# Order of batch 1's theta stage, three more conversion buffers and separate last stores in a fused attention and mixing kernel

## The chip, the cores and the metric

The kernel runs on one core of one Trainium2 chip. The metric is the device time of one execution in microseconds (us), lower is better. The core's engines are TensorE (PE in the rows, with PEld for its weight loads), VectorE (DVE), ScalarE (ACT), GpSimd (POOL) and SyncE (SP), which here only issues DMA transfers. Each engine works through its own list of instructions in order; semaphores make one wait for another.

## What is computed

The reference has three parts, one behind the other, on two batches of 768 tokens with 512 channels (8 heads of 64). Its core:

```python
def _attn_ref(q, k, v, proj):          # q, k, v: [2, 8, 768, 64]
    q_bucket = bits of (q @ proj > 0); k_bucket = bits of (k @ proj > 0)
    scores = where(q_bucket == k_bucket, q @ k.T / sqrt(D), -1e9)
    return softmax(scores) @ v
def _moe_ref(x, w_ch1, w_ch2):
    u = x + real(fft(fft(x, axis=1), axis=2))
    un = (u - mean(u)) / sqrt(var(u) + 1e-06)
    return u + relu(un @ w_ch1) @ w_ch2
def _moe2_ref(x, w_theta, w_tok_r, w_tok_i, w_ch):
    theta = x @ w_theta
    zr, zi = x * cos(theta), x * sin(theta)
    y = w_tok_r @ zr + w_tok_i @ zi    # over the 768 tokens
    u = x + y
    return u + relu(u @ w_ch)
```

The weights of the last two parts are float64 in the inputs, the result is float32.

## The kernel before

**Staging.** Attention of batch 0, then attention of batch 1 beside the Fourier sums and the MLP of batch 0, then those of batch 1 beside the `theta` stage of batch 0, and at the end the late stages, which the change is about: the last MLP group `mlp2(1, 2)`, the `theta` stage of batch 1, and the token sums and channel products of both batches in halves of 384 output tokens. Matrix products are made from a high and a low half of each operand (`h` and `l` at the end of a name), three products for one.

**Order.** Nobody writes the engines' lists by hand. Each stage is a Python generator; `timed(gen, t0, dt)` (L910) runs it and gives each of its steps a priority, a due time of `t0` plus `dt` for each step, through `at(us)` (L131), and the tile scheduler of the language (L1167) merges all steps into one list for each engine, by its own simulation of time. `sooner(us)` makes some steps due earlier, here the update of `u` at the end of `mlp2`. `t0 = T["m1"] + 124` (L1041) is the due time at which the late stages start.

**theta (L814).** For each of 6 tiles t of 128 tokens PE transposes the tile of `u` into PSUM (`psf`); ACT copies it to `xs`, which SP stores to a DRAM buffer `xT` for later, and to the high half `xh`; DVE makes the low half `xl` by a subtraction. Twelve matmuls with `wthh` and `wthl` give theta in PSUM. Then come `nn` (ACT, POOL: the number of whole turns), `rr` (DVE, POOL: the rest), two sines on ACT, and the products zr and zi with their halves in the buffers named `x`, `u`, `za`, `zb`, `zc`. Tiles t = 2 and t = 5 of batch 1 need the update of `u` at the end of `mlp2(1, 2)`: `u<-psm,u` on DVE.

**Conversion of weights (from_f64 L169, conv32 L191, conv_tok L1016).** A chunk of a float64 weight is loaded by SP into a buffer `r64` (`r` in the rows) of a ring `cvs`; two ACT steps (`r<-r,chalf` and `r<-r`) and one DVE step make float32 of it; ACT copies the high half (`w1h`, `wtx` or `wchh`) and POOL subtracts for the low half (`w1l`). The ring has `NCV = 3` buffers, so the load of a chunk waits until the chunk three before it has been used by ACT and POOL. The token weights have 12 chunks of 384 columns for each half of the output tokens (`conv_tok(0)`, `conv_tok(1)`), `wch` has four of 512.

**tok_sum (L855) and tok_out (L889).** The first makes a half's token sums: 36 matmuls for each of four channel blocks, in `psm` or `psf`, added to `xt`, which is loaded back from `xT`. The second multiplies by `wch`, adds the relu (`xt<-psm,xt` on DVE) and stores two channel blocks of `xt` at a time.

**Late calls and their due times.** The last two chunks of half 0 at t0 − 14; `theta(1)` at t0; `tok_sum(0, 0)` at t0 + 20; `wch` at t0 + 22; `tok_sum(1, 0)` at t0 + 40 beside the chunks of half 1; `tok_out(0, 0)` at t0 + 56; the rest up to `tok_out(1, 1)` at t0 + 90 and `tok_out(0, 1)` at t0 + 100.

Of the kernel before, what the change touches and what calls it, by code (L numbers as in the profile page):

```python
# [9 lines left out]
F32 = mybir.dt.float32  # L10
# [5 lines left out]
AF = mybir.ActivationFunctionType  # L16
# [17 lines left out]
def f(t):  # L34
    return t.bitcast(F32)
# [35 lines left out]
def fused_kernel(ctx, tc, A, out):  # L71
# [3 lines left out]
    def pool(name, bufs=1, **kw):  # L75
        return tc.alloc_tile_pool(name=name, bufs=bufs, **kw)
# [10 lines left out]
    def stt(eng, out, in0, in1, op, scale=1.0):  # L87
# [5 lines left out]
    T = dict(  # L93
        pet='dpd', dup=1, c2=0, c0=46, cx=0, wm=6, gf=1, o2=0, xs=1, sb=2, al=[['p', 2], ['p2', 3], ['pt', 3]], cs='v', g0=1,
        lg=[[0, 2], [2, 4], [4, 6]], ub=2, pace0=1.6, lead=60, f0=50.0, w1=60.0, w1s=1.0, b1=115, pace1=2.6,
        w2=100.0, w2s=1.0, m0=170.0, f1=190.0, th=240.0, m1=290.0, z0=330.0, wt=300.0, n0=8, n1=16, k0=12, k1=16, c1=46, i0=40, i1=[20, 10],
        ne=42, es=150, ld='ss', lc='s', ps=[[0, 3], [0, 5], [1, 0], [1, 5]])
    P3 = ((0, 0), (0, 1), (1, 0))

# [714 lines left out]
    def theta(b, wth, zt):  # L814
        x2 = u_t[b]
        for t in range(NT):
            c = slice(128 * t, 128 * t + 128)
            pt = PS1()
            for kd in range(4):
                PE.transpose(pt[:, 128 * kd:128 * kd + 128], x2[:, t, 128 * kd:128 * kd + 128], ident)  # L820
            xs = zt([128, 4, 128], F32, "xs")
            AC.activation(out=xs, in_=pt.rearrange("p (k n) -> p k n", k=4), func=AF.Copy)
            SY.dma_start(out=xTd[b][:, :, c], in_=xs)
            xh = zt([128, 4, 128], F32R, "xh")
            xl = zt([128, 4, 128], F32R, "xl")
            pk = pt.rearrange("p (k n) -> p k n", k=4)
            AC.activation(out=xh, in_=pk, func=AF.Copy)
            V.tensor_tensor(out=xl, in0=pk, in1=f(xh), op=ALU.subtract)
            xx = (xh, xl)
            th = PS1()  # L830
            n = 0
            for kd in range(4):
                for a, k in P3:
                    mm(th, xx[a][:, kd], wth[k][:, kd], n == 0, n == 11)
                    n += 1
            nn = zt([128, DM], F32, "nn")
            AC.activation(out=nn, in_=th, func=AF.Identity, scale=1.0 / TWO_PI, bias=c_mag)
            PL.tensor_scalar(out=nn, in0=nn, scalar1=1.0, scalar2=-MAGIC, op0=ALU.mult, op1=ALU.add)
            rr = zt([128, DM], F32, "rr")
            V.scalar_tensor_tensor(out=rr, in0=nn, scalar=-PC1, in1=th, op0=ALU.mult, op1=ALU.add)  # L840
            V.scalar_tensor_tensor(out=rr, in0=nn, scalar=-PC2, in1=rr, op0=ALU.mult, op1=ALU.add)
            PL.tensor_scalar(out=rr, in0=rr, scalar1=3.1415925, scalar2=-3.1415925, op0=ALU.min, op1=ALU.max)
            V.tensor_scalar(out=nn.bitcast(U32), in0=rr.bitcast(U32), scalar1=0x7FFFFFFF, scalar2=None, op0=ALU.bitwise_and)
            AC.activation(out=rr, in_=rr, func=AF.Sin)
            AC.activation(out=nn, in_=nn, func=AF.Sin, scale=-1.0, bias=c_pi2)
            for r, trig in enumerate((nn, rr)):
                stt(V if r else PL, trig, trig, x2[:, t], ALU.mult)
                zh, zl = z_t[b][r]
                AC.activation(out=zh[:, t], in_=trig, func=AF.Copy)
                stt(PL if r else V, zl[:, t], trig, f(zh[:, t]), ALU.subtract)  # L850
            yield
# [34 lines left out]
            split(ps, kd)  # L886
            yield

    def tok_out(b, half, wch, kx):  # L889
        c = slice(TH * half, TH * half + TH)  # L890
        xt, uh, ul = kx
        uu = (uh, ul)
        for m in range(4):
            ps = PS1()
            n = 0
            for kd in range(4):
                for k, a in P3:
                    mm(ps[:, 0:TH], wch[k][:, kd, 128 * m:128 * m + 128], uu[a][:, kd], n == 0, n == 11)
                    n += 1
            V.scalar_tensor_tensor(out=xt[:, m], in0=ps[:, 0:TH], scalar=0.0, in1=xt[:, m], op0=ALU.max, op1=ALU.add)  # L900
            if m % 2:
                SY.dma_start(out=out[b, 128 * m - 128:128 * m + 128, c].rearrange("(k p) t -> p k t", p=128),
                             in_=xt[:, m - 1:m + 1])
            yield
# [90 lines left out]
    def zt(shape, dt, tag):  # L995
        n = turn.get(tag, 0)
        turn[tag] = n + 1
        return mk(zts[n % len(zts) if tag in ("nn", "rr") else 0], shape, dt, tag)
# [27 lines left out]
    ln_p.release()  # L1026
    m_p.release()
    w2_p.release()
    z1_p = pool("z1")
    z_t[1] = [[zz(u0_p, "u"), zz(z1_p, "za")], [zz(z1_p, "zb"), zz(z1_p, "zc")]]  # L1030
    wx_p = pool("wx")
# [9 lines left out]
    t0 = T["m1"] + 124  # L1041
    timed(conv_tok(0, 10), t0 - 14, 1)
    now[0] = "f"
    timed(theta(1, wth, zt), t0, 1)
    now[0] = "m"
    k0 = operands(xt_p, xt_p)
    timed(tok_sum(0, 0, wt, k0), t0 + 20, 2)
# [19 lines left out]
    timed(tok_sum(0, 1, wt, k1), t0 + 80, 2)  # L1067
    now[0] = "f"
    timed(tok_out(1, 1, wch, k0), t0 + 90, 1)
    timed(tok_out(0, 1, wch, k1), t0 + 100, 1)  # L1070
    for p in (xt1_p, wc_p, zb_p, u1_p, xt_p, wx_p, z1_p, dr_p, ring["f"][0][0], ring["m"][1][0], ring["m"][0][0], w1_p, x_p, u0_p, cv_p, const):
        p.release()


# [99 lines left out]
```

## Time and profile before

| | us |
|---|---|
| median of 3 runs | 740.17 (737.42 to 740.52) |
| the profiled execution | 742.22 |
| span in its profile | 740.5 |
| PE busy | 672.8 |
| PE weight loads busy (beside PE) | 515.0 |
| DVE busy | 401.4 |
| ACT busy | 376.4 |
| POOL busy | 371.2 |

The profile records one execution. Its own time is 742.22 us; the span from the first to the last recorded instruction is 740.5 us, with a mean granted clock of 0.965. A row of the timeline gives start, duration, engine, line, operation, written tile, read tiles and shape; in square brackets stands the idle time of the engine just before and what ended it. Nearly all instructions come from two helper lines, L62 and L64, so the tile names tell what an instruction is. Buffer numbers are left out in the rows (`r_6585` is `r`) but not in the order listings below. A "x2" behind a row means two like instructions in a row. The late stages are the last 190 us or so.

### The profile page before, as it was taken

How to read it: one execution, taken by the hardware profiler on the slowest of the kernel's cores; microseconds unless marked ns; L12 is line 12 of the kernel's file. 1: busy time of each engine (PE TensorE's matmuls, PEld its weight loads, DVE VectorE, ACT ScalarE, POOL GpSimd, SP SyncE). 2: the span in 40 equal slices, each digit the busy share in tenths (PEclk: the TensorE clock that was granted, in tenths of full speed). 3: DMA queues.
4: the chain of work that ended last, by engine and by line, in shares of the span. 5: the costliest groups of instructions: out<-in, count | busy, mean ns of one | idle time of the engine just before them, and what ended most of it. 6: DMA issues, size and time to landing. Idle time of an engine off the chain costs nothing.

```text
span 740.5 us, 13468 instructions
## 1 busy us (share of the span) xinstructions
PE 672.8 (91%) x5424; PEld 515.0 (70%) x5424; DVE 401.4 (54%) x649; ACT 376.4 (51%) x603; POOL 371.2 (50%) x312
## 2 busy tenths in 40 slices
PE   5798988778868897999999999999999799989997
PEld 2365566666747654786687675686584798989997
DVE  1466777778899556642394871254321366552222
ACT  2465554867898788764222260354325555562000
POOL 2777879589687888885450110134313155831000
PEclk9999999969789999999999999999999999999999
DMA  9886867469799999786550160010005511561202
GB/s 331 183 167 145 154 115 143 97 176 202 194 227 232 237 235 263 153 142 117 107 175 1 29 165 1 15 43 15 1 2 152 181 44 30 178 185 49 86 1 85
DMA packets 161438, 93.69 MB, mean 127 GB/s; under 512 B 137056, under 2 KB 147552, under 8 KB 161376
## 3 DMA queue, kind: packets, MB, share of 16 engines
q1 hardware_dynamic: 159440, 86.27, 49.9%
q0 software_dynamic: 1936, 6.57, 2.5%
q8 instruction: 42, 0.69, 0.4%
q14 instruction: 20, 0.16, 0.1%
HBM read 49.82 MB, written 6.29 MB: 76 GB/s over the span
## 4 chain that ended last, share of the span: by engine, by line
PE 42%; issue 10%; POOL 10%; DMA 9%; ACT 6%; DVE 4%; SPq 0%; POOLq 0%; ACTq 0%; DVEq 0%
PE psm L62 28%; PE psf L62 10%; DMA r<-in_wtok 4%; DMA r<-in_w 2%; POOL w1l L62 2%; ACT r L62 2%; POOL p L62 2%; PE pss L62 2%; POOL pt L62 2%; PE pso L62 2%; DMA r<-in_wch 1%; DMA x<-p 1%; ACT p L62 1%; ACT stk L62 1%; POOL w2l L62 1%
## 5 line engine op out<-in xcount | busy, mean ns | idle before, releaser
L62 PE MATMUL psm<-unT,w1h 128*128 128x256 f16 x768 | 130.1, 274 | 1.6 <-DVE u L62 1.4
L62 DVE SCALAR_TENSOR_TENSOR r<-r 128x512 uint32<-128x512 uint32 (+1 forms) x64 | 66.7, 1047 | 73.3 <-ACT r L62 61.4
L62 PE MATMUL psm<-unT,w1l 128*128 128x256 f16 x384 | 105.1, 274 | 0.0
L62 PEld LDWEIGHTS <-w1h 128*128 128x128 f16 (+1 forms) x774 | 75.2, 98 | 17.2 <-issue 6.3
L62 POOL TENSOR_TENSOR w1l<-r,w1h 128x384 fp32r<-128x384 f32 (+1 forms) x36 | 41.4, 1163 | 59.0 <-ACT w1h L62 58.9
L62 PEld LDWEIGHTS <-hh 128*128 128x128 f16 x384 | 36.9, 98 | 42.7 <-issue 1.1
L62 ACT ACTIVATE r<-r,chalf 128x512 uint32<-128x512 uint32 (+1 forms) x64 | 46.1, 721 | 38.3 <-DMA r<-in_wtok 20.5
L64 PE MATMUL pss<-stk 64*128 64x384 f32 (+1 forms) x288 | 58.4, 492 | 5.9 <-ACT p L64 3.0
L62 PE MATMUL pss<-stk 128*128 128x384 f32 x192 | 50.0, 388 | 11.9 <-ACT stk L62 6.6
L62 POOL TENSOR_TENSOR p<-p,p 128x768 f16<-128x768 f32 x32 | 53.4, 1672 | 12.9 <-ACT p L62 11.4
L62 PE MATMUL psm<-w2h,hl 128*128 128x512 f16 x192 | 59.7, 380 | 0.0
L62 PE MATMUL psm<-w2l,hh 128*128 128x512 f16 x192 | 59.4, 379 | 0.0
L62 PE MATMUL psm<-w2h,hh 128*128 128x512 f16 x192 | 59.3, 380 | 0.0
L62 DVE TENSOR_REDUCE nm<-pss 128x1 f32<-128x768 f32 x48 | 44.9, 946 | 20.5 <-PE pss L62 20.4
L64 DVE TENSOR_REDUCE nm<-pss 128x1 f32<-128x768 f32 x48 | 43.6, 950 | 22.5 <-PE pss L64 22.5
L62 ACT ACTIVATE p<-pss,nm 128x768 f32<-128x768 f32 x48 | 42.7, 895 | 21.7 <-DVE nm L62 20.2
L62 DVE SCALAR_TENSOR_TENSOR hl<-psm,hh 128x512 f16<-128x512 f32 x48 | 32.9, 685 | 37.8 <-ACT hh L62 37.7
L62 ACT ACTIVATE hh<-psm 128x512 f16<-128x512 f32 x48 | 28.3, 590 | 46.5 <-PE psm L62 46.4
L62 PEld LDWEIGHTS pss<-stk 128*128 128x128 f32 x192 | 35.3, 209 | 15.8 <-ACT stk L62 7.7
L62 PEld LDWEIGHTS <-w1l 128*128 128x128 f16 x384 | 37.6, 98 | 6.4 <-issue 1.7
L62 ACT ACTIVATE r<-r 128x512 f32<-128x512 f32 (+1 forms) x64 | 39.6, 619 | 0.0
L62 POOL TENSOR_SCALAR nn<-nn 128x512 f32<-128x512 f32 x12 | 8.3, 691 | 60.9 <-ACT nn L62 60.9
(319 smaller groups left out, 1583.8 us busy)
## 6 DMA issues: line engine op xcount, KB each, us to landing
r<-in_w SPq DMA_DIRECT2D x32, 512.0 KB, 4.9
r<-in_wtok SPq DMA_DIRECT2D x24, 384.0 KB, 3.8
vr<-in_v SPq DMA_DIRECT2D x8, 390.0 KB, 3.7
stk<-stk SPq DMA_DIRECT2D x16, 192.0 KB, 3.7
xT<-xs SPq DMA_DIRECT2D x12, 256.0 KB, 2.6
xt<-xT SPq DMA_DIRECT2D x4, 768.0 KB, 5.1
out<-xt SPq DMA_DIRECT2D x8, 384.0 KB, 2.5
ct<-in_ct POOLq DMA_DIRECT2D x4, 579.0 KB, 7.7
```

The lines of the kernel that those rows point to most:

```text
L62: return fn(*a, **k)
L64: self.last = fn(*a, **k)
```

## The change

Five edits, four of them in the late stages:

1. In `theta`, `xh` and `xl` are written ahead of `xs` and its store (for both batches).
2. `theta(1)` is due at t0 − 16 instead of t0 (`tp=16`), which is ahead of the last two chunks of half 0.
3. Once the MLP's weights `w2` are released, three more `r64` buffers join the ring (`cv3`); the last chunks of half 0, `wch` and the chunks of half 1 use a ring of six.
4. `tok_out(0, 1)`, the last stage, stores each of its four channel blocks by itself (four transfers of 128 x 384 float32) instead of two and two.
5. The scratch in which POOL's DMA descriptors are written is set to 4096 instead of the default, which frees SBUF.

```diff
...
-        w2=100.0, w2s=1.0, m0=170.0, f1=190.0, th=240.0, m1=290.0, z0=330.0, wt=300.0, n0=8, n1=16, k0=12, k1=16, c1=46, i0=40, i1=[20, 10],
+        w2=100.0, w2s=1.0, m0=170.0, f1=190.0, th=240.0, m1=290.0, z0=330.0, wt=300.0, n0=8, n1=16, k0=12, k1=16, c1=46, tp=16, i0=40, i1=[20, 10],
...
             pt = PS1()
             for kd in range(4):
                 PE.transpose(pt[:, 128 * kd:128 * kd + 128], x2[:, t, 128 * kd:128 * kd + 128], ident)
-            xs = zt([128, 4, 128], F32, "xs")
-            AC.activation(out=xs, in_=pt.rearrange("p (k n) -> p k n", k=4), func=AF.Copy)
-            SY.dma_start(out=xTd[b][:, :, c], in_=xs)
             xh = zt([128, 4, 128], F32R, "xh")
             xl = zt([128, 4, 128], F32R, "xl")
             pk = pt.rearrange("p (k n) -> p k n", k=4)
             AC.activation(out=xh, in_=pk, func=AF.Copy)
             V.tensor_tensor(out=xl, in0=pk, in1=f(xh), op=ALU.subtract)
+            xs = zt([128, 4, 128], F32, "xs")
+            AC.activation(out=xs, in_=pt.rearrange("p (k n) -> p k n", k=4), func=AF.Copy)
+            SY.dma_start(out=xTd[b][:, :, c], in_=xs)
             xx = (xh, xl)
             th = PS1()
             n = 0
...
             split(ps, kd)
             yield
 
-    def tok_out(b, half, wch, kx):
+    def tok_out(b, half, wch, kx, last=False):
         c = slice(TH * half, TH * half + TH)
         xt, uh, ul = kx
         uu = (uh, ul)
...
                     mm(ps[:, 0:TH], wch[k][:, kd, 128 * m:128 * m + 128], uu[a][:, kd], n == 0, n == 11)
                     n += 1
             V.scalar_tensor_tensor(out=xt[:, m], in0=ps[:, 0:TH], scalar=0.0, in1=xt[:, m], op0=ALU.max, op1=ALU.add)
-            if m % 2:
+            if last:
+                SY.dma_start(out=out[b, 128 * m:128 * m + 128, c], in_=xt[:, m])
+            elif m % 2:
                 SY.dma_start(out=out[b, 128 * m - 128:128 * m + 128, c].rearrange("(k p) t -> p k t", p=128),
                              in_=xt[:, m - 1:m + 1])
             yield
...
     ln_p.release()
     m_p.release()
     w2_p.release()
+    cv3_p = pool("cv3", 3)
+    cvs += [cv3_p] * 3
     z1_p = pool("z1")
     z_t[1] = [[zz(u0_p, "u"), zz(z1_p, "za")], [zz(z1_p, "zb"), zz(z1_p, "zc")]]
     wx_p = pool("wx")
...
     t0 = T["m1"] + 124
     timed(conv_tok(0, 10), t0 - 14, 1)
     now[0] = "f"
-    timed(theta(1, wth, zt), t0, 1)
+    timed(theta(1, wth, zt), t0 - T["tp"], 1)
     now[0] = "m"
     k0 = operands(xt_p, xt_p)
     timed(tok_sum(0, 0, wt, k0), t0 + 20, 2)
...
     timed(tok_sum(0, 1, wt, k1), t0 + 80, 2)
     now[0] = "f"
     timed(tok_out(1, 1, wch, k0), t0 + 90, 1)
-    timed(tok_out(0, 1, wch, k1), t0 + 100, 1)
-    for p in (xt1_p, wc_p, zb_p, u1_p, xt_p, wx_p, z1_p, dr_p, ring["f"][0][0], ring["m"][1][0], ring["m"][0][0], w1_p, x_p, u0_p, cv_p, const):
+    timed(tok_out(0, 1, wch, k1, True), t0 + 100, 1)
+    for p in (xt1_p, wc_p, zb_p, u1_p, xt_p, wx_p, z1_p, cv3_p, dr_p, ring["f"][0][0], ring["m"][1][0], ring["m"][0][0], w1_p, x_p, u0_p, cv_p, const):
         p.release()
 
 
...
     import concourse.bacc as _bacc
     from concourse.bass_utils import run_bass_kernel_spmd as _run
 
-    nc = _bacc.Bacc("TRN2", target_bir_lowering=False, num_devices=1)
+    nc = _bacc.Bacc("TRN2", target_bir_lowering=False, num_devices=1, dynamic_dma_scratch_size=4096)
     lay = _layout(inputs)
     arrays, aps = {}, {}
     for name, a in lay.items():
```

The scheduler moves other steps with these. On ACT, around the end of `mlp2(1, 2)`, the list before reads as follows (`r_6585` is chunk 9 of half 0, `r_6712` and `r_6719` its last two, `r_7143` the first of `wch`):

```order
L62 ACTIVATE r_6585<-r_6585,chalf 128x384
L62 ACTIVATE r_6585<-r_6585 128x384
L62 ACTIVATE r_6712<-r_6712,chalf 128x384
L62 ACTIVATE r_6712<-r_6712 128x384
L62 ACTIVATE w1h<-r_6585 128x384
L62 ACTIVATE r_6719<-r_6719,chalf 128x384
L62 ACTIVATE r_6719<-r_6719 128x384
L62 ACTIVATE wtx<-r_6712 128x384
L62 ACTIVATE wtx<-r_6719 128x384
L62 ACTIVATE xs<-psf 128x512
L62 ACTIVATE xh<-psf 128x512
L62 ACTIVATE r_7143<-r_7143,chalf 128x512
```

The same place of ACT in the changed kernel, where `r_7146` and `r_7153` are the first two of `wch`:

```order
L62 ACTIVATE r_6585<-r_6585,chalf 128x384
L62 ACTIVATE r_6585<-r_6585 128x384
L62 ACTIVATE nn<-psf,cmag 128x512
L62 ACTIVATE xh<-psf 128x512
L62 ACTIVATE r_7146<-r_7146,chalf 128x512
L62 ACTIVATE w1h<-r_6585 128x384
L62 ACTIVATE r_7146<-r_7146 128x512
L62 ACTIVATE xs<-psf 128x512
L62 ACTIVATE r_7153<-r_7153,chalf 128x512
```

The first `xh` now stands 11 rows ahead of this piece, the second is in it, ahead of its `xs` with steps of `wch` between; the last two chunks of half 0 have moved behind it.

On DVE the update of `u` (`u_5032<-psm,u_5032`) in the list before, from the last two chunks of half 0 on:

```order
L62 SCALAR_TENSOR_TENSOR r_6712<-r_6712 128x384
L62 SCALAR_TENSOR_TENSOR r_6719<-r_6719 128x384
L62 SCALAR_TENSOR_TENSOR u_5032<-psm,u_5032 128x512 x2
L62 TENSOR_TENSOR xl<-psf,xh 128x512
L62 SCALAR_TENSOR_TENSOR r_7143<-r_7143 128x512
L62 SCALAR_TENSOR_TENSOR r_7150<-r_7150 128x512
L62 SCALAR_TENSOR_TENSOR r_7157<-r_7157 128x512
```

And in the changed kernel, from chunk 9 of half 0 on:

```order
L62 SCALAR_TENSOR_TENSOR r_6585<-r_6585 128x384
L62 TENSOR_TENSOR xl<-psf,xh 128x512
L62 SCALAR_TENSOR_TENSOR rr<-nn,psf 128x512
L62 SCALAR_TENSOR_TENSOR rr<-nn,rr 128x512
L62 SCALAR_TENSOR_TENSOR r_7146<-r_7146 128x512
L62 SCALAR_TENSOR_TENSOR r_7153<-r_7153 128x512
L62 TENSOR_SCALAR nn<-rr 128x512
L62 SCALAR_TENSOR_TENSOR rr<-rr,u_5032 128x512
L62 SCALAR_TENSOR_TENSOR r_7160<-r_7160 128x512
L62 SCALAR_TENSOR_TENSOR rr<-nn,psf 128x512
L62 SCALAR_TENSOR_TENSOR u_5032<-psm,u_5032 128x512 x2
```

Three chunks of `wch` and the first steps on theta's `nn` and `rr` now stand ahead of the update of `u`, which stood ahead of the first chunk of `wch`.

SP's loads and stores before, from chunk 9 of half 0 on:

```order
L62 DMA r_6585<-in_wtok 128x768
L62 DMA r_6712<-in_wtok 128x768
L62 DMA r_6719<-in_wtok 128x768
L62 DMA r_7143<-in_wch 128x1024
L62 DMA xt<-xT_129 128x4x384
L62 DMA xT_130<-xs 512x1x128
L62 DMA r_7150<-in_wch 128x1024
L62 DMA r_7157<-in_wch 128x1024
L62 DMA xT_130<-xs 512x1x128 x5
L62 DMA r_7164<-in_wch 128x1024
```

And in the changed kernel:

```order
L62 DMA xT_130<-xs 512x1x128
L62 DMA r_6585<-in_wtok 128x768
L62 DMA r_7146<-in_wch 128x1024
L62 DMA r_7153<-in_wch 128x1024
L62 DMA xT_130<-xs 512x1x128
L62 DMA r_7160<-in_wch 128x1024
L62 DMA r_6715<-in_wtok 128x768
L62 DMA r_6722<-in_wtok 128x768
L62 DMA xt<-xT_129 128x4x384
L62 DMA r_7167<-in_wch 128x1024
L62 DMA r_7340<-in_wtok 128x768
```

The stores to `xT_130` now stand among the loads of `wch`; the load of `xt`, 768 KB, has moved behind three chunks of `wch` and the last two of half 0.

## Rows read from the trace of the kernel before

**Rows 1.** The page: each engine's busy time, share of the span, instructions.

```profile
PE 672.8 (91%) x5424; PEld 515.0 (70%) x5424; DVE 401.4 (54%) x649; ACT 376.4 (51%) x603; POOL 371.2 (50%) x312
```

**Rows 2.** Waits of PE, 410 to 741 us: releaser, us in total, times, longest.

```profile
PE psf L62 <- ACT xh L62: 4.5, 3, 2.2
PE psm L62 <- ACT w1h L62: 2.7, 1, 2.7
...
PE psm L62 <- DVE xt L62: 1.1, 1, 1.1
```

**Rows 3.** Timeline of PE, instructions that ended two of its gaps.

```profile
580.71 0.50 PE L62 MATMUL psf<-wthh,xh 128*128 128x512 f32 x1 [1.87 <-ACT xh L62]
...
667.29 0.44 PE L62 MATMUL psm<-w1h,zb 128*128 128x384 f32 x1 [2.71 <-ACT w1h L62]
```

**Rows 4.** Timeline of ACT, the first tile of batch 1's theta.

```profile
579.59 0.58 ACT L62 ACTIVATE xs<-psf 128x512 f32<-128x512 f32 x1
580.07 0.59 ACT L62 ACTIVATE xh<-psf 128x512 fp32r<-128x512 f32 x1
```

**Rows 5.** Timeline of SP and ACT, chunks of the token weights' second half.

```profile
659.63 2.74 SPq L62 DMA_DIRECT2D r<-in_wtok  x3
...
665.74 0.63 ACT L62 ACTIVATE r<-r,chalf 128x384 uint32<-128x384 uint32 x1 [1.76 <-DMA r<-in_wtok]
```

**Rows 6.** Timeline of PE: mlp2's first matmul, transposes after its last, token matmuls, theta's end.

```profile
552.50 0.38 PE L62 MATMUL psm<-w2h,hh 128*128 128x512 f16 x1
...
573.22 0.49 PE L62 MATMUL psf<-ident,u 128*128 128x128 f32 x3
...
574.25 0.34 PE L62 MATMUL psm<-w1l,zb 128*128 128x384 f32 x1
...
575.29 0.34 PE L62 MATMUL psm<-w1l,zb 128*128 128x384 f32 x1
...
583.92 0.28 PE L62 MATMUL psf<-ident,u 128*128 128x128 f32 x1
```

**Rows 7.** Timeline of ACT: a chunk's two steps, and nn.

```profile
573.49 0.65 ACT L62 ACTIVATE r<-r,chalf 128x384 uint32<-128x384 uint32 x1 [1.39 <-DMA r<-in_wtok]
574.04 0.54 ACT L62 ACTIVATE r<-r 128x384 f32<-128x384 f32 x1
...
590.27 0.68 ACT L62 ACTIVATE nn<-psf,cmag 128x512 f32<-128x512 f32 x1
```

**Rows 8.** Timeline of SP and ACT: loads of wch chunks and their first steps.

```profile
578.38 0.33 SPq L62 DMA_DIRECT2D r<-in_wch  x1
...
580.83 1.41 SPq L62 DMA_DIRECT2D r<-in_wch  x2
...
582.16 0.75 ACT L62 ACTIVATE r<-r,chalf 128x512 uint32<-128x512 uint32 x1 [1.50 <-DMA r<-in_wch]
...
587.83 0.77 ACT L62 ACTIVATE r<-r,chalf 128x512 uint32<-128x512 uint32 x1 [4.37 <-DMA r<-in_wch]
```

**Rows 9.** Timeline of DVE and POOL: steps of theta and the update of u.

```profile
579.02 1.28 DVE L62 SCALAR_TENSOR_TENSOR u<-psm,u 128x512 f32<-128x512 f32 x2
...
591.11 0.62 POOL L62 TENSOR_SCALAR nn<-nn 128x512 f32<-128x512 f32 x1 [10.15 <-ACT nn L62]
...
591.76 0.69 DVE L62 SCALAR_TENSOR_TENSOR rr<-nn,psf 128x512 f32<-128x512 f32 x1
```

**Rows 10.** The page's DMA issues: tiles, count, KB each, us to landing.

```profile
xT<-xs SPq DMA_DIRECT2D x12, 256.0 KB, 2.6
...
out<-xt SPq DMA_DIRECT2D x8, 384.0 KB, 2.5
```

**Rows 11.** POOL's queue: the page's packets, one kind of load, POOL's step after them.

```profile
q0 software_dynamic: 1936, 6.57, 2.5%
...
sn<-in_sn POOLq DMA_DIRECT2D x4, 576.0 KB, 8.6
...
20.60 0.82 POOL L64 TENSOR_SCALAR p<-p 128x768 f16<-128x768 f32 x1 [7.04 <-ACT p L64]
```

## The prediction

> **What bounds the kernel now.** I read the busy times first: TensorE (PE) is busy 91% of the span [rows 1], so only its gaps can be won. The waits of PE from 410 us on come next, because everything that the diff moves runs after that: three gaps end with `xh` (4.5 us together, the longest 2.2), one with a token chunk `w1h` (2.7) and one with `xt` (1.1) [rows 2]. The timeline places them: the first `xh` gap ends at 580.71, the chunk gap at 667.29 [rows 3]. Together they are 4.5 + 2.7 + 1.1 = 8.3 us; everywhere else in this stretch PE is fed. At its end PE runs gap-free into the last stores. So the question is which of the 8.3 us the change removes, and what it starts instead.
>
> Why PE waits there. `xh` of batch 1's first token tile stands on ScalarE (ACT) behind the copy `xs` for the store, and both behind the last token chunks: `xs` starts at 579.59, `xh` at 580.07, 0.48 us later, and PE starts 0.64 after that [rows 3, 4]. Of that gap 0.48 is the order xs/xh, the rest is theta coming late. The chunk gap is a load chain: with three buffers `r64`, SyncE (SP) issues three chunk loads as one bundle at 659.63, ACT's first step on one of them starts only at 665.74, and PE starts 1.5 us after that [rows 3, 5].
>
> **The change, part by part.**
>
> *xh ahead of xs, theta earlier by 16 us.* Nothing is added or removed: ACT, VectorE (DVE), PE do the same steps in another order. PE takes two of the six theta tiles inside the last mlp2 block now. That block is 96 matmuls between 552.50 and 573.22 [rows 6], 20.72/96 = 0.216 us each. Twelve theta matmuls with three transposes take 583.92 − 580.71 = 3.2 us [rows 3, 6]; a token matmul takes (575.29 − 574.25)/6 = 0.173 [rows 6]. The old waits of tiles t=0 and t=1 (1.87 of [rows 3] among the 4.5) go, because PE has mlp2 matmuls to do meanwhile. Two waits replace them.
>
> First new wait, S1. In the new order PE does 59 mlp2 matmuls (552.50 + 12.7 = 565.2), tile t=0 with its transposes (some 3.5, to 568.7), 28 more mlp2 matmuls (6.05, to about 574.8), and then tile t=1, which needs its `xh`. On ACT that `xh` stands behind both steps of chunk r_6585, which is load-bound as before, and behind `nn`: the steps start at 573.49 and 574.04 and end at 574.58; `nn` takes 0.68, of which the next step overlaps some 0.1 as these two do [rows 7], and `xh` 0.59 [rows 4], so 575.7. S1 = 575.7 − 574.8 = **0.9 us**; bounds 0.5 (the chunk's load issues as much earlier as its predecessors do) and 2.0 (one more chunk step of 0.65 and 0.54 comes between [rows 7]).
>
> Second new wait, S2. The rest of tile t=1 (2.8), the last 8 mlp2 matmuls (1.7) and 26 token matmuls (4.5) bring PE from 575.7 to about 585.1. There stand the transposes of tile t=2, whose `u` DVE must have updated. On DVE this update stood ahead of the chunks of wch; now three of these (r_7146, r_7153, r_7160) and an `rr` stand ahead of it. The last of them is what counts: r_7160's load stands on SP behind the store of t=1's `xs`. ACT does xh (to 575.7), r_7146 when it has landed (about 576.4) with `w1h` between its steps, then `xs` to 578.7; SP issues the store and the load at about 579.3. How long the load takes is the open price: 582.16 − 578.38 = 3.8 us for one wch chunk, 587.83 − 580.83 = 7.0 for another, which was issued behind a 768 KB transfer [rows 8]. No such transfer stands ahead now, but two chunk loads and a store do, so I take 4.4, near the lower row: it lands at 583.7. Then two ACT steps and `nn` (some 0.65 each by [rows 7, 8], to 585.6), 0.62 on GpSimd (POOL), 0.6 for `rr`, 0.6 for the first of two `u` [rows 9]: 587.5. S2 = 587.5 − 585.1 = **2.5 us**, bounds 1.9 and 5.1.
>
> After that PE has other work ready whenever a tile is late: by the same working xh of t=3 has about 1 us of slack and the later tiles 3 us or more, so the third `xh` wait goes too. Removed here: 4.5; added: 3.4.
>
> *Three more chunk buffers.* The load chain behind the 2.7 us wait is cut: chunks of the second half can be issued six ahead. Followed forward as for S2, with landings of 3.8 us [rows 8], the chunks of the second half are converted some 12 us before PE takes them, where they had no slack. The DVE wait behind `xt` (1.1) was DVE's queue held by the same late chunks; it goes with them. Removed: 3.8. The buffers cost no instruction. They need room in SBUF, hence the smaller scratch for POOL's DMA descriptors; I cost that at nothing, since POOL's queue moves 1,936 packets in the whole run [rows 11], 121 for each of 16 engines (see rival C).
>
> *Single last stores.* Two stores of 384 KB become four of half that. Behind the last DVE step then lies one store of 192 KB instead of 384 KB. A 384 KB store lands in 2.5 us, one of 256 KB (`xT`) in 2.6 [rows 10]: by these rows size hardly matters. I take −0.3 us, bounds 0 and −1.2 (landing in proportion to the bytes). Two more issues on SP lie beside PE's last matmuls. The Trainium skill ("DMA: Bandwidth & Descriptors", Anatomy of one DMA — SWDGE (gpsimd) path) gives a fixed 2.0 us and bytes over 436 GB/s for a DMA of another path; for 393 KB that is an estimate of 2.9 where the row shows 2.5, and halving the bytes would save 0.45, which would make the sum 0.15 us lower.
>
> *Sum.* −4.5 − 3.8 + 0.9 + 2.5 − 0.3 = **−5.2 us**. The profiled execution took 742.22 us (span 740.5 and 1.7 around it), 2.05 above the median of the runs, so 737.0 for it and 740.17 − 5.2 = **735.0** for the median.
>
> **The rivals.** A is the sum above.
>
> B, the wch loads land late: r_7160 takes the 7.0 us of [rows 8], S2 becomes 5.1, and tile t=3 loses its slack too, for some 0.7. New waits 0.9 + 5.1 + 0.7 = 6.7, so −8.3 + 6.7 − 0.3 = −1.9: **738.3**. For it: five loads and stores are now bunched in 7 us there. Against: the 7.0 had the 768 KB transfer ahead of it, which now comes later.
>
> C, slower: the smaller scratch makes POOL stall at the start, where it issues its loads in one go. If its ring could hold only some of them, a load would wait for an earlier one to land: four waits of 8.6 us [rows 11] = 34, less the 7.04 us that POOL sat idle before 20.60 [rows 11] = 27 us late for the attention steps behind it, **762**. It decides once the ring holds fewer packets than these loads need. Against: the whole run puts 121 packets on an engine. The Trainium skill ("SBUF — State Buffer", SBUF size: 192, 224, or 256?) puts the usual scratch at 16 KiB, and "DMA: Bandwidth & Descriptors" (Terms) a descriptor at 16 bytes; a quarter of it would hold an estimated 256 of them, by which C would not occur; no run here shows it yet.
>
> D, the buffers don't do it: the second half's chunks stay late because ACT and DVE, not the loads, hold them. The 3.8 us stay: −5.2 + 3.8 = −1.4, **738.8**. Against: before the gap ACT sits idle 1.76 us for a load, not for an engine [rows 5].
>
> **How the numbers follow.** A 0.58, B 0.24, D 0.10, C 0.08. Prediction 735.0. A alone spans 733.1 (S1 0.5, S2 1.9, tail −1.2) to 737.5 (S1 2.0, S2 3.9); the runs of before differ by 3 us among themselves, so I add about 1 us on either side and reach to B and D above: 732.0 to 740.0, which leaves C and a little more out. Half a per cent, 3.7 us, is about what a measurement of this kernel can tell from no change; faster by more means under 736.5. Most of A lies there (0.56), its rest, B and D lie within (0.35), C and an S2 that is far longer lie above (0.09).
>
> **What would show it.** In the changed kernel's PE waits from 410 on: no wait on `w1h` near 655 to 665 and none on `xt` (else D); one short wait on `xh` near 575 (S1), one on `u` near 585 to 588 of 2 to 3 us (S2; 5 would be B), and none on `xh` later. PE's last matmul should end near 731. On POOL the stretch 9 to 21 us should look as before, with the steps behind its loads starting at 20.6 (else C). The last store should be 192 KB and land in 2.0 to 2.5 us. The prediction is wrong if a landing there is over 12 us (S1 + S2 then eat the whole gain), if PE runs dry again in the token sums, or if the scheduler's order turned out late somewhere in the stage of tile t=3, where my slack is smallest.

## The result: 1.0% faster, and the profile after

The changed kernel takes 732.71 us (732.02 to 734.45, 6 runs) against 740.35 us of the kernel before (737.42 to 741.93, 6 runs): a ratio of 0.9898, interval 0.9874 to 0.9923. That is 7.6 us where 5.2 were forecast, 732.7 against 735.0, inside the range of 732 to 740. A second set of runs of the same kernel (`after2` below) gave 0.9931, interval 0.9897 to 0.9965, or 5.1 us; the two intervals share 0.9897 to 0.9923, so some 5 to 7.5 us is what can be said.

The profiled execution took 733.24 us, its span is 731.5. PE's waits from 440 us on, as engine, tile and line, releaser, us in total, times, longest (before: [rows 2]):

```profile
PE psf L62 <- DVE u L62: 2.7, 1, 2.7
PE psf L62 <- ACT xh L62: 0.2, 1, 0.2
```

All 8.3 us of old waits are gone, and two waits stand in their place, on the tiles that the forecast named. The timeline of PE shows where (before: [rows 3]):

```profile
572.09 0.50 PE L62 MATMUL psf<-wthh,xh 128*128 128x512 f32 x1 [0.19 <-ACT xh L62]
584.38 1.12 PE L62 MATMUL psf<-ident,u 128*128 128x128 f32 x4 [2.70 <-DVE u L62]
```

The first is the second theta tile waiting for its `xh` (S1), the second is the transposes of tile t=2 waiting for the update of `u` (S2). The chain behind S2, from SP's, ACT's and DVE's timelines (before: [rows 8, 9]):

```profile
575.45 0.52 SPq L62 DMA_DIRECT2D xT<-xs  x1
576.07 0.58 SPq L62 DMA_DIRECT2D r<-in_wch  x1
...
580.42 0.75 ACT L62 ACTIVATE r<-r,chalf 128x512 uint32<-128x512 uint32 x1 [1.43 <-DMA r<-in_wch]
581.07 0.65 ACT L62 ACTIVATE r<-r 128x512 f32<-128x512 f32 x1
581.62 0.67 ACT L62 ACTIVATE nn<-psf,cmag 128x512 f32<-128x512 f32 x1
...
581.76 0.69 DVE L62 SCALAR_TENSOR_TENSOR r<-r 128x512 uint32<-128x512 uint32 x1 [2.65 <-ACT r L62]
583.03 0.69 DVE L62 SCALAR_TENSOR_TENSOR rr<-nn,psf 128x512 f32<-128x512 f32 x1 [0.58 <-POOL nn L62]
583.64 1.28 DVE L62 SCALAR_TENSOR_TENSOR u<-psm,u 128x512 f32<-128x512 f32 x2
```

Read it downwards: SP issues the store of `xs`, then the load of r_7160 at 576.07; ACT starts on it at 580.42, 4.35 us later; `nn` follows on ACT; DVE does the chunk, waits 0.58 for `nn`, does `rr`, and only then updates `u`. Every link is in the order in which the forecast put it.

**The clock behind the wait.** The wait on `u` costs more than its 2.7 us, which the forecast left out. Two rows of the windows view (a stretch, its length, the busy times of PE, PEld, DVE, ACT and POOL, then the granted clock, the DMA share and GB/s), and two of PE's token matmuls:

```profile
580.00:583.00 3.00, 1.67 (x10) 1.35 (x8) 0.69 (x1) 2.58 (x5) 0.98 (x2) 1.00 0.97 350
584.00:587.00 3.00, 2.62 (x10) 2.63 (x11) 3.00 (x6) 1.68 (x4) 1.49 (x2) 0.50 0.40 158
...
585.61 0.52 PE L62 MATMUL psm<-w1h,zb 128*128 128x384 f32 x1
587.38 0.34 PE L62 MATMUL psm<-w1h,zb 128*128 128x384 f32 x1
```

PE had stood idle for 2.70 us; from 584 to 587 us the granted clock is 0.50 (1.2 GHz), before and behind it 1.00 (2.4 GHz). The seventh token matmul behind the transposes starts 2.82 us after them (584.38 to 587.20). In `rot_tp20` below, where the same transposes come without a wait and at a clock of 1.00, it starts 1.48 us after them (581.08 to 582.56), so the slower clock costs 1.3 us here. In `after2`, behind a wait of 1.9 us, the clock is 0.50 from 583.2 to 586.4, and ten matmuls start 0.32 us apart instead of 0.174, some 1.5 us. Not every wait is followed by this: behind the 2.71 us of [rows 3] the clock of the kernel before stays at 1.00.

**A yardstick for the late stages.** The instruction lists are the same up to about 430 us, yet the changed kernel was 3.1 us earlier there already. Runs of one kernel differ by several us in that front part, so the experiments below are compared by what lies behind a fixed point: the start of the MLP matmul that ends the wait on `u` near 430 us. In the kernel before, in the changed one and in the kernel before profiled once more (`before_b`) that row is:

```profile
431.74 0.38 PE L62 MATMUL psm<-unT,w1h 128*128 128x256 f16 x2 [1.43 <-DVE u L62]
```

```profile
428.60 0.38 PE L62 MATMUL psm<-unT,w1h 128*128 128x256 f16 x2 [1.47 <-DVE u L62]
```

```profile
433.22 0.38 PE L62 MATMUL psm<-unT,w1h 128*128 128x256 f16 x2 [1.43 <-DVE u L62]
```

From here on "late stages" means the span minus this time, which takes in more than the last 190 us that the name stood for above: 740.5 − 431.74 = 308.8 before, 731.5 − 428.60 = 302.9 after, so −5.9 us.

How far one profile can be trusted is seen in four more whose late lists, but for the last store, are those of the kernel before (`before_b`, `scratch`, `scratch_b`, `store4`). Their waits on `xh` come to 3.6, 3.6, 2.3 and 3.0 us, where [rows 2] has 4.5; those on `w1h` and `xt` together to 3.5, 3.6, 3.5 and 3.7, where it has 3.8. So the 8.3 us of waits are 5.8 to 8.3 over the five.

### The profile page after: what moved, and what is told of

It is laid out like the page before. It is cut to its first block, busy times and chain, and to the rows that moved or that the text cites. A ratio compares the mean times of both kernels' runs of the same rounds, so it can differ in the third digit from the quotient of the medians.

```text
span 731.5 us, 13457 instructions
## 1 busy us (share of the span) xinstructions
PE 666.6 (91%) x5424; PEld 512.4 (70%) x5424; DVE 404.6 (55%) x649; ACT 374.9 (51%) x603; POOL 372.1 (51%) x312
## 4 chain that ended last, share of the span: by engine, by line
PE 46%; POOL 11%; issue 9%; DMA 8%; ACT 5%; DVE 4%; SPq 0%; POOLq 0%; ACTq 0%; DVEq 0%
PE psm L62 30%; PE psf L62 14%; DMA r<-in_w 3%; POOL p L62 3%; POOL w1l L62 3%; DMA x<-p 2%; ACT r L62 2%; POOL pt L62 2%; POOL stk L62 1%; ACT stk L62 1%; POOL w2l L62 1%; PE pso L62 1%; PE pss L62 1%; ACT p L62 1%; DMA r<-in_wtok 1%
## 5 line engine op out<-in xcount | busy, mean ns | idle before, releaser
L62 PE MATMUL pss<-stk 128*128 128x384 f32 x192 | 51.5, 396 | 10.5 <-ACT stk L62 5.9
L64 PE MATMUL pss<-stk 64*128 64x384 f32 (+1 forms) x288 | 54.4, 463 | 6.7 <-ACT p L64 3.2
L62 POOL TENSOR_TENSOR stk<-tt,stk 64x768 fp32r<-64x768 f32 x16 | 31.5, 1971 | 9.9 <-issue 8.7
```

The lines of the kernel that those rows point to most:

```text
L62: return fn(*a, **k)
L64: self.last = fn(*a, **k)
```

## The experiments

| label | what differs | late stages, us | ratio to before, interval |
|---|---|---|---|
| before | | 308.8 | |
| before_b | the kernel before again | 307.5 | 1.0014, 0.9993 to 1.0035 |
| scratch | edit 5 alone | 309.1 | 1.0010, 0.9981 to 1.0039 |
| scratch_b | edit 5 alone, again | 307.7 | 1.0005, 0.9975 to 1.0035 |
| store4 | edit 4 alone | 307.8 | 1.0019, 0.9997 to 1.0042 |
| order12 | edits 1 and 2 alone | 305.4 | 0.9980, 0.9955 to 1.0005 |
| bufs35 | edits 3 and 5 alone | 304.2 | 0.9964, 0.9934 to 0.9993 |
| after | all five | 302.9 | 0.9898, 0.9874 to 0.9923 |
| after2 | all five, again | 302.0 | 0.9931, 0.9897 to 0.9965 |
| no2 | all but edit 2 | 301.9 | 0.9928, 0.9899 to 0.9956 |
| tp8 | all, theta 8 us earlier instead of 16 | 305.3 | 0.9954, 0.9929 to 0.9978 |
| tp20 | all, theta 20 us earlier | 302.1 | 0.9902, 0.9870 to 0.9934 |
| rot_tp16 | all, ring of buffers turned | 301.2 | 0.9899, 0.9862 to 0.9937 |
| rot_tp20 | both of the last two | 299.6 | 0.9865, 0.9830 to 0.9900 |

The four profiles without a change in the late lists (before, before_b, scratch, scratch_b) spread from 307.5 to 309.1 (mean 308.3), so a difference of one profile under about 1.5 us says little by itself; the waits inside say more. Two expectations took this scatter too small: `before_b` was to have 308.8 give or take 0.5 and has 307.5, `after2` was to have 302.9 give or take 0.3 and has 302.0.

### scratch, scratch_b and before_b: is the front faster?

```diff
-    nc = _bacc.Bacc("TRN2", target_bir_lowering=False, num_devices=1)
+    nc = _bacc.Bacc("TRN2", target_bir_lowering=False, num_devices=1, dynamic_dma_scratch_size=4096)
```

> The kernel before with edit 5 alone (the smaller scratch), every engine's list as before. The changed kernel reached the point at 430 us 3.1 us earlier than the kernel before although its lists are the same up to there; the late stages gave 5.9 us. Theory S (the scratch or the addresses it moves makes the front faster): this kernel is 2 to 3 us faster than before (ratio 0.996 to 0.997), and its first MLP matmul that waits for u starts near 428.6. Theory R (the front's gain is scatter from run to run): ratio 1.000 within 0.002, and that matmul starts near 431.7 give or take 2.

> The kernel before with the smaller scratch alone, a second time. The point at 430 us came at 427.3 to 429.9 us in the nine profiles with the small scratch and at 431.4 to 434.2 in the three with the default one, yet the timed runs of the small scratch alone were level with before. Theory S (the scratch makes the front 2 to 4 us faster): again near 428.7 in the profile, and a ratio of 0.995 to 0.997. Theory R (scatter): ratio 1.000 give or take 0.003, and the point anywhere between 427 and 434.

> The kernel before itself, once more with a profile, to see how far two profiles and two sets of runs of one kernel lie apart. Theory S: the point at 430 us comes at 431.4 or later. Theory R: it comes anywhere between 427 and 434. Late stages 308.8 give or take 0.5 by both, ratio 1.000 give or take 0.003.

The timed runs say no twice (1.0010 and 1.0005; the lower ends of the intervals, 0.9981 and 0.9975, leave room for 1.4 and 1.9 us). The profiles say something else: the point at 430 us came at 428.72 and 427.91 with the small scratch, at 433.22 for the kernel before again, and over all experiments at 427.3 to 429.9 in ten profiles with the small scratch and at 431.4 to 434.2 in the four with the default one. In the profile of scratch_b, 737.35 us, the kernel was 3.3 us under the median of its own timed runs, 740.64. What sets the profiled executions apart stays open (the mean granted clock up to 427 us does not: it is 0.94 in both profiles of the kernel before and in both of the small scratch); what is shown is that the small scratch is worth nothing that 12 timed runs against 33, and 12 against 23, can see.

Rival C, a stall of POOL at the start, is refuted: after its seven loads POOL goes on at 18.39 us in the changed kernel, after 6.11 us of idle time with the same releaser as in [rows 11].

```profile
18.39 0.83 POOL L64 TENSOR_SCALAR p<-p 128x768 f16<-128x768 f32 x1 [6.11 <-ACT p L64]
```

That agrees with the estimate in the forecast from the Trainium skill ("SBUF — State Buffer", SBUF size: 192, 224, or 256?, and "DMA: Bandwidth & Descriptors", Terms), by which a quarter of the scratch holds an estimated 256 descriptors and C does not occur; no run shows at which size it would.

### store4: the tail

```diff
-            if m % 2:
+            if last:
+                SY.dma_start(out=out[b, 128 * m:128 * m + 128, c], in_=xt[:, m])
+            elif m % 2:
```

> Edit 4 alone (four stores of 192 KB at the end instead of two of 384 KB). In the traces the time from the start of the last DVE step to the end of the span was 4.3 us before and 3.5 us after. If the smaller store makes that: 0.5 to 0.8 us faster, tail 3.5 us. If landing does not depend on the size: 0, tail 4.3.

The last DVE step starts at 735.75 and the span ends at 739.2, a tail of 3.45 us; before it was 740.5 − 736.25 = 4.25, and with all edits 731.5 − 727.99 = 3.5. Over all fourteen profiles the tail is 4.2 to 4.3 us in the six with the stores of before and 3.4 to 3.5 in the eight with edit 4. The last DVE step and the stores from 700 us on (KB each, median us to landing) here (before: 384 KB, 2.5 us in [rows 10]), and the last DVE step in the changed kernel, whose 192 KB stores land in 1.9 us too:

```profile
735.75 0.56 DVE L62 SCALAR_TENSOR_TENSOR xt<-psf,xt 128x384 f32<-128x384 f32 x1 [1.53 <-PE psf L62]
...
out<-xt SPq DMA_DIRECT2D x2, 384.0 KB, 2.4
out<-xt SPq DMA_DIRECT2D x4, 192.0 KB, 1.9
```

```profile
727.99 0.56 DVE L62 SCALAR_TENSOR_TENSOR xt<-psf,xt 128x384 f32<-128x384 f32 x1 [1.52 <-PE psf L62]
```

So the smaller last store takes 0.75 to 0.8 us off the end of the trace, 0.5 of it by landing sooner; the rest is not accounted for. The timed runs don't show it: 1.0019, interval 0.9997 to 1.0042, leaves room for 0.2 us. The kernel before came at 1.0014 against itself (`before_b`), so such sets of runs are off by more than the effect. The Trainium skill ("DMA: Bandwidth & Descriptors", Anatomy of one DMA — SWDGE (gpsimd) path) let 0.45 be estimated for half the bytes, which agrees with the 0.5 between the landings here and is nearer than my 0.3.

### order12 and bufs35: the two large parts alone

Edits 1 and 2 without the buffers, and the buffers (edits 3 and 5) without these:

```diff
-            xs = zt([128, 4, 128], F32, "xs")
...
             V.tensor_tensor(out=xl, in0=pk, in1=f(xh), op=ALU.subtract)
+            xs = zt([128, 4, 128], F32, "xs")
...
-    timed(theta(1, wth, zt), t0, 1)
+    timed(theta(1, wth, zt), t0 - 16, 1)
```

> Edits 1 and 2 alone (xh ahead of xs, theta 16 us earlier), three chunk buffers as before. By the prediction's terms: the xh waits of 4.5 us go, a wait of 0.2 to 0.9 us on xh and one on u near 585 us come, and the waits on w1h (2.7) and xt (1.1) stay. With the u wait at 2.7 us as in the changed kernel: 1 to 1.6 us faster (ratio 0.998). Rival: with only three buffers the wch chunk ahead of the u update is loaded later, the u wait is 5 us or more and the edits alone are no gain or a loss (ratio 1.000 to 1.003).

```diff
     w2_p.release()
+    cv3_p = pool("cv3", 3)
+    cvs += [cv3_p] * 3
...
+    nc = _bacc.Bacc("TRN2", target_bir_lowering=False, num_devices=1, dynamic_dma_scratch_size=4096)
```

> Edits 3 and 5 alone (three more chunk buffers, which need the smaller scratch). By the prediction: the waits on w1h and xt (3.8 us) go, the three xh waits (4.5) stay: 3.8 us faster (ratio 0.995). If the smaller scratch gives 2 to 3 us at the front by itself, 6 to 7 us (0.991). Rival D (ACT and DVE, not the loads, hold the chunks): no gain, the w1h wait stays above 2 us.

Waits of PE from 440 us on, order12:

```profile
PE psm L62 <- DVE xt L62: 1.7, 2, 1.0
PE psf L62 <- ACT xh L62: 1.0, 2, 0.7
PE psf L62 <- DVE xl L62: 0.8, 1, 0.8
PE psf L62 <- DVE u L62: 0.6, 1, 0.6
PE psm L62 <- POOL wtx L62: 0.5, 1, 0.5
```

and bufs35:

```profile
PE psf L62 <- ACT xh L62: 2.0, 2, 1.3
PE psm L62 <- ACT wtx L62: 1.1, 1, 1.1
PE psf L62 <- DVE xl L62: 0.6, 1, 0.6
```

By its waits order12 did more than its term in the sum; the rival's wait on `u` of 5 us or more did not come (0.6). The wait of 2.7 us on `w1h`, which was to stay, is gone too, though the ring has three buffers: the loads of half 1 start earlier, presumably because theta is out of the way earlier. SP's long run of them begins at 634.28 here, 200.1 us behind the fixed point (434.20 in this profile), and at 642.37 in the kernel before, 210.6 behind it:

```profile
634.28 24.97 SPq L62 DMA_DIRECT2D r<-in_wtok  x10
```

```profile
642.37 12.37 SPq L62 DMA_DIRECT2D r<-in_wtok  x6
```

With bufs35 the waits on `w1h` and `xt` are gone, as expected, with 1.1 on `wtx` in their place. Its 2.0 us on `xh` (and 0.6 on `xl`) are not clearly below the 2.3 to 4.5 of the unchanged lists, so no gain there is shown.

The parts overlap: the wait on `w1h`, 2.3 to 2.7 us in all five profiles with unchanged late lists, goes with either of the two large ones alone. The late stages roughly agree in size, though each figure is one profile: against the mean of 308.3 they gain 2.9 (order12), 4.1 (bufs35) and, from the tail, 0.8 (store4), together 7.8, and all five edits gain 5.4 to 6.3. The timed runs are too coarse for it (1.5 us for order12, as expected, 2.7 for bufs35, where 3.8 were expected). The forecast's split (−1.1 net for the order, −3.8 for the buffers) adds up to about the right total without being the split.

Rival D is refuted by bufs35: no wait on `w1h` is left. In the changed kernel the last loads of half 1 are issued by 638.5; before, loads were issued up to 662 [rows 5]. POOL finishes the chunk that is converted last (`wtx`) at 648.65, and PE takes it at 657.78, 9 us later (the forecast said some 12 of slack). SP, POOL and PE in the changed kernel:

```profile
629.06 9.43 SPq L62 DMA_DIRECT2D r<-in_wtok  x6
...
646.13 2.52 POOL L62 TENSOR_TENSOR wtx<-r,wtx 128x384 fp32r<-128x384 f32 x2 [1.96 <-ACT wtx L62]
...
657.78 0.51 PE L62 MATMUL psm<-wtx,u 128*128 128x384 f32 x2
```

### no2 and after2: is edit 2 worth anything?

```diff
-    timed(theta(1, wth, zt), t0 - T["tp"], 1)
+    timed(theta(1, wth, zt), t0, 1)
```

> The changed kernel again (all five edits), beside the next three on one chip. The late stages are measured from the start of the matmul that ends the wait on u near 430 us to the end of the span: 308.8 us before, 302.9 in the changed kernel, 305.4 with edits 1 and 2 alone, 304.2 with 3 and 5 alone, 307.8 with 4 alone. If the 3.1 us that the changed kernel gained ahead of 430 us were scatter of the front, this run again has 302.9 give or take 0.3 in the late stages, and the median against before is 6 us faster (ratio 0.992) rather than 7.6; if they belong to the change, 7.6 us again (0.990).

> The changed kernel without edit 2 (theta of batch 1 due at t0 as before). Theory of the prediction (edit 2 removes the lateness of theta's first tiles that edit 1 cannot): xh waits of 1.3 us or more near 576 us stay as with edits 3 and 5 alone, less 0.48 us each; the u wait of 2.7 near 584 goes, since the update of u stands ahead of r_7160 again. Late stages 302.5 to 303.5. Rival (edit 2 is worth nothing beside the others, it trades its xh waits for the wait on u): late stages 302.0 or less, that is as fast as the changed kernel or faster.

Waits of PE in no2 from 440 us on:

```profile
PE psf L62 <- ACT xh L62: 1.4, 1, 1.4
PE psf L62 <- DVE xl L62: 0.8, 1, 0.8
PE psm L62 <- ACT wtx L62: 0.4, 1, 0.4
```

2.6 us, against 1.9 (after2) and 2.9 (after) with edit 2; late stages 301.9 against 302.0 and 302.9; ratios 0.9928 and 0.9931 on one chip. The rival held, though by only 0.1 us of its bound: beside the other edits, theta 16 us earlier trades the `xh` and `xl` waits for the wait on `u` and gains nothing that can be measured. Its wait also costs the slower clock behind it, while no2's granted clock is 1.00 from 440 to 720 us. My theory for this run was wrong in its size (302.5 to 303.5); of the waits it named those on `xh` and `u` rightly and missed the 1.2 us on `xl` and `wtx`.

after2 repeats the changed kernel's late stages within 0.9 us, and its median gain, 734.85 against 739.92, is 5.1 us.

### tp8 and tp20: what makes the wait on u?

```diff
-    timed(theta(1, wth, zt), t0 - T["tp"], 1)
+    timed(theta(1, wth, zt), t0 - 8, 1)
```

(with − 20 in tp20)

> The changed kernel with theta of batch 1 only 8 us earlier instead of 16: on DVE the update of u then stands ahead of the third chunk of wch (r_7160), and no theta tile is inside mlp2. If it is that chunk that makes the u wait, the wait of 2.7 us is gone (under 0.3 left) and the late stages take 300.2 to 301.5 us, with a short xh wait at the first theta tile. If the wait comes from elsewhere, a wait on u of over 2 us stays.

> The changed kernel with theta of batch 1 20 us earlier: two theta tiles inside mlp2 at earlier places, and the update of u again ahead of r_7160. If that chunk makes the u wait: the wait is gone or under 0.5, late stages 300.2 to 301 us. If the earlier theta only moves the shortage (chunks of half 0 late behind theta's steps): new waits on xh or w1h of 1 us or more, late stages near 302 or more.

In both, the update of `u` stands ahead of r_7160 on DVE, and in both the wait on `u` is gone or nearly (none, and 0.3). But the loss stays: the late stages take 305.3 and 302.1 us where 300.2 to 301.5 were expected if the chunk were all. In tp8 PE waits 3.6 us for `xh`, 3.2 of it at once. SP's and ACT's timelines show the same load under a new name:

```profile
576.63 0.58 SPq L62 DMA_DIRECT2D r<-in_wch  x1
...
581.44 0.74 ACT L62 ACTIVATE r<-r,chalf 128x512 uint32<-128x512 uint32 x1 [4.23 <-DMA r<-in_wch]
...
584.17 0.57 ACT L62 ACTIVATE xh<-psf 128x512 fp32r<-128x512 f32 x1
```

ACT stood still for 4.23 us for this load, with `xh` of the next theta tile queued five steps behind it. Besides, tp8 loses by the clock: behind the 3.2 us it is 0.50 from 584 to 590, and the first and last of twelve theta matmuls start 5.5 us apart (584.80 to 590.30) instead of 3.0 (580.71 to 583.68 in the kernel before, at 1.00). In tp20 the waits are, from 440 us on:

```profile
PE psm L62 <- ACT wtx L62: 2.0, 1, 2.0
PE psf L62 <- ACT xh L62: 0.9, 1, 0.9
PE psf L62 <- DVE u L62: 0.3, 1, 0.3
```

So r_7160 on DVE is what PE saw as the wait on `u`. In the changed kernel and in tp8 the cause lies a step further back: one late load blocks an in-order engine, and whatever stands behind it there becomes the wait's name. For tp20 this is not shown: ACT begins with the chunks of `wtx` at 584.64 without waiting for a load, and its last stop ahead of them is for POOL's `nn`, so there the order of ACT's steps holds them at least as much as the load. SP and ACT in tp20:

```profile
578.61 0.90 SPq L62 DMA_DIRECT2D r<-in_wtok  x2
...
581.86 0.63 ACT L62 ACTIVATE u<-nn 128x512 fp32r<-128x512 f32 x1 [1.39 <-POOL nn L62]
...
584.64 0.63 ACT L62 ACTIVATE r<-r,chalf 128x384 uint32<-128x384 uint32 x1
```

### rot_tp20 and rot_tp16: issue that load earlier

```diff
     cvs += [cv3_p] * 3
+    turn["cv"] += 3
```

The ring is advanced by three places when the new buffers join, and nothing else is touched (rot_tp20 has theta 20 us earlier besides); the scheduler merges the lists anew. The expectation of rot_tp20 names the buffers the wrong way round: by the order in which the ring is gone through, the last two chunks of half 0 and the fourth of `wch` (r_7167) take the three old buffers now, which come free one by one as chunks of half 0 are done; the first three of `wch` take the new ones, whose place in SBUF is that of the weights that mlp2 still reads. In the changed kernel it is the other way: r_7146, r_7153 and r_7160 in the old ones, the last two chunks of half 0 in the new ones.

> The changed kernel with theta of batch 1 20 us earlier (as in the run before) and the ring of six advanced by three places when the new buffers join, so that the last two chunks of half 0 and the first of wch take the new buffers and SP issues all three ahead of the second store of theta. With theta 20 us earlier PE lost 2.0 us for the converted chunk wtx, 0.9 for xh and 0.3 for u. Theory (the place of a chunk in the ring sets when its load is issued, and that load ends the wait): the wtx wait falls below 0.5 us, late stages 300.0 to 300.8 us, ratio to before 0.986 to 0.990. Rival (ACT and DVE have too many steps there, whichever chunk comes first): a wait of 2 to 3 us stays under another name, late stages 301.5 to 302.5.

> The changed kernel with the ring alone advanced by three places: on SP the third chunk ahead of the update of u (now r_7167) is issued ahead of the second store of theta, on DVE one of the two updates of u stands directly behind it and the rr step behind that. Theory (the load issued behind that store makes the u wait): the wait on u falls from 1.9 to 2.7 us to 1.2 us or less, late stages 300.5 to 301.5. Rival (the wait is set by the chunk's buffer coming free at the end of the conversion before it, not by the store): the wait stays at 1.9 us or more, late stages 302 to 303.

In rot_tp20 SP issues three chunks in a row at 568.47:

```profile
568.47 2.72 SPq L62 DMA_DIRECT2D r<-in_wtok  x3
```

(chunk 9 of half 0 and the two of `wtx`), where tp20 issues `wtx`'s two at 578.61, some 8 us later as seen from the fixed point. PE's only wait left from 440 us on is

```profile
PE psm L62 <- POOL wtx L62: 0.5, 1, 0.5
```

and the late stages take 299.6 us, the shortest of all; 731.57 against 740.86 us, ratio 0.9865, interval 0.9830 to 0.9900. In rot_tp16 the wait on `u` fell to 0.8, with 0.5 and 0.5 for two other tiles, late stages 301.2. The theory's expectation held for rot_tp16, and nearly for rot_tp20 (a wait of 0.53 where "below 0.5" was said, late stages 0.4 us under the range); neither rival's waits came. So the place of a chunk in the ring counts. That it counts by the time of the load's issue alone is not shown, since the engines' orders changed with it. In rot_tp20 ACT does the chunks of `wtx` from 573.37 on, ahead of all of `wch`; in tp20 it does them behind three of these. In rot_tp16 the load ahead of the update of `u` is issued at 574.80, 145.8 us behind the fixed point, where r_7160 in the changed kernel comes 147.5 behind it, 1.6 us earlier; but the `rr` step has moved too:

```profile
580.62 0.69 DVE L62 SCALAR_TENSOR_TENSOR r<-r 128x512 uint32<-128x512 uint32 x1 [2.50 <-ACT r L62]
581.23 0.68 DVE L62 SCALAR_TENSOR_TENSOR u<-psm,u 128x512 f32<-128x512 f32 x1
581.90 0.69 DVE L62 SCALAR_TENSOR_TENSOR rr<-nn,psf 128x512 f32<-128x512 f32 x1
```

The first update of `u` stands 0.6 us behind the chunk instead of 1.9. So it starts 2.8 us earlier as seen from the fixed point, 1.5 by the load and 1.3 by the place of `rr`, for a wait that is 1.1 to 1.9 us shorter. Whether the store ahead of r_7160 on SP or its buffer coming free held the load is not told apart either, since both changed. The intervals of rot_tp20 and of the changed kernel overlap in part; by the waits left (0.5 against 1.9 to 2.9 us) rot_tp20 is the better of the two by 1.4 to 2.4 us, by the late stages by 2.4 to 3.3. What lies between, some 1 us, is about what the slower clock behind the wait on `u` costs: in rot_tp20 the granted clock is 1.00 from 560 to 720 us.

## Why the prediction was right, step by step

| step of the forecast | forecast, us | after | after2 |
|---|---|---|---|
| waits on xh | −4.5 | −4.3 | −4.5 |
| waits on w1h and xt | −3.8 | −3.8 | −3.8 |
| S1, xh of tile t=1 | +0.9 | (in the first row) | 0 |
| S2, u for tile t=2 | +2.5 | +2.7 | +1.9 |
| tail | −0.3 | −0.7 | −0.8 |
| clock of 0.50 behind S2 | 0 | +1.3 | +1.5 |
| sum of these | −5.2 | −4.8 | −5.7 |
| late stages, against the profile of before (308.8) | | −5.9 | −6.8 |
| late stages, against the mean of four (308.3) | | −5.4 | −6.3 |

The first row of "after" holds the 0.2 that is left on `xh`, which is S1.

**The removed waits** went as forecast, all of them. Their size is in part luck: the 4.5 us on `xh` that the forecast took from one profile is the highest of five with unchanged late lists (2.3 to 4.5, mean 3.4), so about 1 us less was to be had there. (From 410 us on the forecast calls PE fed everywhere else; it passed over the 1.43 us on `u` at 431.74, which no edit touches.) The buffers' mechanism (loads issued earlier) was right; that the order alone frees the same chain was not in the forecast, and rests on order12.

**S2** was right in place and chain, and the wait in size. The working has a slip that hardly matters: 575.7 + 2.8 + 1.7 + 4.5 is 584.7, not 585.1, and 587.5 − 585.1 is 2.4; in the trace PE came at 581.68, or 584.8 in the time of the kernel before. What the forecast left out is the slower clock behind the wait, 1.3 to 1.5 us more. The load was taken at 4.4 us between bounds of 3.8 and 7.0; in the profile it is 580.42 − 576.07 = 4.35, so rival B (7.0) did not occur. The store of `xs` and the load were forecast for about 579.3 in the time of the kernel before; they came at 575.45 and 576.07, with this execution 3.1 us earlier at the fixed point.

**S1** was too large: 0.9 forecast, 0.2 and 0 measured. The step that failed is the assumption that chunk r_6585 on ACT stays as late as before. In the changed kernel its two steps start at 569.90 and 570.45; 3.1 us added for the earlier front, that is 573.0 and 573.55, 0.5 earlier than the 573.49 and 574.04 in [rows 7]. The lower bound of 0.5 us rested on that very reason and was still too high, as PE came 0.2 to 0.3 us later than I had it.

```profile
569.90 0.64 ACT L62 ACTIVATE r<-r,chalf 128x384 uint32<-128x384 uint32 x1 [1.01 <-DMA r<-in_wtok]
570.45 0.53 ACT L62 ACTIVATE r<-r 128x384 f32<-128x384 f32 x1
570.88 0.67 ACT L62 ACTIVATE nn<-psf,cmag 128x512 f32<-128x512 f32 x1
571.45 0.58 ACT L62 ACTIVATE xh<-psf 128x512 fp32r<-128x512 f32 x1
```

**The tail** was too small, 0.3 against 0.7 to 0.8. I judged by medians, 2.5 us for 384 KB and 2.6 for 256 KB of another transfer; the row that mattered is that of the 192 KB stores themselves, which land in 1.9 instead of 2.4.

**The sum.** The late stages gained 5.4 to 6.8 us where 5.2 were forecast, so the forecast of 735.0 was 0.2 to 1.6 us too high by them. That it came so near is in part luck: the `xh` term of one profile and the clock, put at nothing, made the forecast gain too large, and S1, the tail and about 1 us that no row of waits shows (−5.9 against −4.8, −6.8 against −5.7) made it too small. Where that 1 us lies was not found.

**The rest of the 7.6 us**, some 1 to 2 us, lies ahead of 430 us, where no step of the change is at work that the timed runs can show; the second set of runs (5.1 us) does not have it. It is scatter between sets of runs, as far as it can be told.

## What to carry to other kernels

A late load on an in-order engine shows up under the name of whatever is queued behind it: before moving the named step, follow the chain back, to the DMA if there is one, and ask what set the time of its issue and its place in the lists (here both changed with the buffer that a chunk was given). Look at the granted clock behind a wait as well: here, in three runs, 1.9 to 3.2 us of waiting cost 1.3 to 2.5 us more. Edits that feed the same chain overlap, so measure each alone and all but one before adding up terms; here one of five was worth nothing beside the others. When the effect is 1% and the front of the program scatters by as much, compare traces from a fixed instruction behind the scatter.

## What was not expected

Two profiles of the kernel before reached the same instruction at 431.74 and 433.22 us, and ten of kernels with a smaller scratch at 427.3 to 429.9, while the timed runs of before and of the smaller scratch alone were level within 0.4%; why the profiled executions part in this way was not found. And splitting the last 384 KB store took 0.75 us off the end, where the landings (2.4 and 1.9 us) differ by 0.5.
